# One opening load of an attention kernel issued from ScalarE's queue instead of SyncE's

## The chip, the cores and the metric

The kernel runs on one core of one Trainium2 chip. The metric is the device time of one execution in microseconds (us), given as the median of several executions. Times "at 2.73 us" are counted from the start of the profiled span. TensorE, which does the matrix multiplications, is called PE in the profile, VectorE DVE, ScalarE ACT, GpSimd POOL and SyncE SP. SPq and ACTq are the sequencers of SyncE and ScalarE, which issue loads; the 16 DMA engines then move a load's rows in packets, each engine a part of them. PSUM is the memory into which TensorE writes its results. PE begins at half its pace (two 256-column matmuls start 0.213 us apart, later 0.109), until the trace shows the full clock granted. ScalarE's "table load" brings in the tables for its functions. "Landing" is the time at which the last of a load's 16 semaphore events came in the trace, so that its reader may start.

## The reference, cut to what matters

Two independent problems, A and B, of the same shape (bf16 inputs; 32 query heads over 4 key/value heads):

```python
B, Sq, D = 16, 32, 1024            # 512 tokens of 1024 features
Hq, Hkv, Sk, Dh = 32, 4, 512, 128
q = (x @ wq)                       # 512 x 1024 times 1024 x 4096
scores = einsum("bhqd,bhkd->bhqk", q, k) * Dh ** -0.5
o = softmax(scores) @ v
out = o @ wo                       # A and B side by side
```

The case is about the first part of `x @ wq` of problem A alone. The contraction over 1024 features goes in eight chunks of 128; a chunk's weight rows are a 128 x 4096 matrix, of which one head takes 128 columns, or 256 bytes of each row.

## The kernel before: the opening

Six heads are begun first, chunk by chunk. x comes in as tokens by features and has to be transposed: chunks 0 to 3 by TensorE, the rest by transposing loads. All loads go through SyncE's queue.

```python
NF = REP - 2                       # 6 heads begun first; TT = 4 token tiles
nc.scalar.preload_act_table_set("natural_log_exp_and_others")
load_x(0, 0, TT // 2)              # x chunks 0-1, first half of the tokens, 128 KB
load_x(0, TT // 2, TT)             # ... second half, 128 KB
load_w0(0, 1, 0, NF // 2)          # chunk 0, heads 0-2, 96 KB   <- the load of the change
load_w0(0, 1, NF // 2, NF)         # chunk 0, heads 3-5, 96 KB
load_w0(1, 2, 0, NF)               # chunk 1, heads 0-5, 192 KB  ("chunk 1's rows")
load_x(2, 0, TT)                   # x chunks 2-3, 256 KB
load_w0(2, 3, 0, NF)               # chunk 2's rows
load_w0(3, 4, 0, NF)               # chunk 3's rows
...                                # more loads
warm_up(22)                        # 22 matmuls on constants, so that PE is not idle
for k, ts in enumerate(((0, TT // 2), (TT // 2, TT))):
    transpose_x(0, *ts, nc.vector.tensor_copy)
    transpose_x(1, *ts, nc.scalar.copy, spare[k])
for ts in ((0, TT // 2), (TT // 2, TT)):
    first_heads(range(0, NF // 2), (0,), *ts)      # six matmuls of 256 columns
first_heads(range(NF // 2, NF), (0,))              # three of 512 columns
first_heads(range(0, NF - 2), (1,))                # four of 512: wait for chunk 1's rows
transpose_x(2, 0, TT, nc.vector.tensor_copy)       # wait for x chunks 2-3
transpose_x(3, 0, TT, nc.scalar.copy)
...                                                # the rest of the kernel
```

## Time and profile before

| | before |
|---|---|
| time, median of 3 executions | 343.27 us (343.26 to 343.75) |
| span of the profiled execution | 341.4 us |
| PE busy | 335.0 us, 98% |
| only PE wait for a load in the opening that the page marks on a matmul | 0.4 us, for chunk 1's rows |

The page of the kernel before, its part 1 (busy time and share of the span) and the head of its part 4 (the chain of work that ended last, by engine):

```profile
PE 335.0 (98%) x2082; PEld 213.2 (62%) x2121; DVE 265.6 (78%) x336; ACT 185.8 (54%) x209; POOL 46.7 (14%) x206
...
PE 94%; DVE 1%; issue 1%; DMA 1%; SPq 1%; ACT 0%; POOL 0%; ACTq 0%
```

PE is busy almost throughout and makes up 94% of the chain, so only the few places where PE stands still can give time back. The next view is the chain of waits of the kernel before in its first 12 us, as start, length and what it was. L477 is the line that loads weight rows, L534 the first heads' matmuls, L524 the transposes of x.

```profile
1.75 0.46 SPq L477
...
2.25 0.43 SPq L477
...
2.73 3.29 DMA w_sb<-in_A_wq_dram
6.02 0.05 issue
6.07 1.04 PE q_ps L534 x4
7.11 0.45 PE xT_ps L524 x8
...
7.61 4.50 PE q_ps L534 x20
```

Read it backwards. The train of matmuls that starts at 7.61 hangs on the four matmuls at 6.07; these waited for a load issued at 2.73 (chunk 1's rows), which took 3.29 us to land, at 6.02. Ahead of it stand SyncE's issues, one after the other; the one at 1.75 is the load that the change moves. PE's own row of the timeline (start, length, what, count), merged over like instructions, for the kernel before:

```profile
3.24 1.06 PE L524 MATMUL xT_ps<-ident,x_sb 128*128 128x128 bf16 x8
4.10 1.60 PE L534 MATMUL q_ps<-xT,w_sb 128*128 128x256 bf16 x9
6.07 1.04 PE L534 MATMUL q_ps<-xT,w_sb 128*128 128x512 bf16 x4 [0.37 <-DMA w_sb<-in_A_wq_dram]
6.94 0.61 PE L524 MATMUL xT_ps<-ident,x_sb 128*128 128x128 bf16 x8
```

The merged row at 4.10 holds the nine matmuls of chunk 0. The ends of matmuls are modelled, so the row seems to end at 5.70; by the distance from start to start (0.216 us for 512 columns) the array is free at 5.54. Until 6.07 it waits 0.53 us. The row at 6.94, the transposes of x chunks 2-3: I call its start **M**.

What the 16 DMA engines did meanwhile, in stretches of half a microsecond (the last two figures of a row are the mean busy share of the DMA engines and the GB/s moved):

```profile
2.00:2.50 0.50, 0.50 (x8) 0.50 (x7) 0.00 (x0) 0.10 (x1) 0.00 (x0) 1.00 0.83 247
...
3.00:3.50 0.50, 0.50 (x8) 0.50 (x6) 0.00 (x0) 0.00 (x0) 0.00 (x0) 1.00 0.65 186
3.50:4.00 0.50, 0.50 (x8) 0.50 (x6) 0.29 (x1) 0.09 (x1) 0.00 (x0) 1.00 0.75 189
4.00:4.50 0.50, 0.50 (x6) 0.40 (x5) 0.29 (x1) 0.45 (x2) 0.00 (x0) 1.00 0.80 230
```

One load, chunk 1's rows, by its issue (engine, count, size, us from issue to landing):

```profile
w_sb<-in_A_wq_dram SPq DMA_DIRECT2D x1, 192.0 KB, 3.3
```

And the end of the kernel before: ScalarE's last copy of a result out of PSUM.

```profile
338.43 0.37 ACT L329 CAST o_sb<-f_ps 128x256 bf16<-128x256 f32 x1 [3.12 <-PE f_ps L320]
```

### The profile page before, as it was taken

Reading aid. Unit: us, or ns where it says so; the run is one execution under the profiler, and the core shown is the slowest. Engines: PE = TensorE matmul, PEld = TensorE weight load, DVE = VectorE, ACT = ScalarE, POOL = GpSimd, SP = SyncE. Lnnn points to the kernel's source line nnn. Section 1 sums busy time; section 2 is a strip of 40 time slices with the busy share of each in tenths; the row PEclk is TensorE's granted clock in tenths of the full one; section 3 lists DMA queues with packets and bytes.
Section 4 is the critical chain, followed back from the end, with each engine's and each line's share of the span. In section 5 each row is a group of like instructions: output and inputs, shape, how many; then the busy total and the mean of one; then the engine's idle time right before and its main releaser. Section 6 shows DMA issues by size and latency. Waiting matters only on the chain.

```text
span 341.4 us, 5454 instructions
## 1 busy us (share of the span) xinstructions
PE 335.0 (98%) x2082; PEld 213.2 (62%) x2121; DVE 265.6 (78%) x336; ACT 185.8 (54%) x209; POOL 46.7 (14%) x206
## 2 busy tenths in 40 slices
PE   8999999999999999999999999999999999999996
PEld 6455666666666666666666666666666666666555
DVE  1046988888988898888888988879888888889540
ACT  3058666666667667666645545555555555555110
POOL 0001110011111111110012221222122101111100
PEclk9999999999999999999999999999999999999999
DMA  6989999999999988999999956999449996340001
GB/s 192 289 166 286 287 219 241 192 198 276 302 282 203 232 231 221 212 302 288 325 274 266 276 135 142 335 256 250 117 109 292 355 206 160 95 113 10 18 18 33
DMA packets 128094, 71.70 MB, mean 210 GB/s; under 512 B 75840, under 2 KB 127296, under 8 KB 128064
## 3 DMA queue, kind: packets, MB, share of 16 engines
q1 hardware_dynamic: 127536, 70.21, 85.3%
q0 software_dynamic: 384, 1.05, 0.8%
q8 instruction: 17, 0.28, 0.3%
q14 instruction: 13, 0.11, 0.1%
q10 hardware_dynamic: 144, 0.07, 0.1%
HBM read 50.86 MB, written 2.10 MB: 155 GB/s over the span
## 4 chain that ended last, share of the span: by engine, by line
PE 94%; DVE 1%; issue 1%; DMA 1%; SPq 1%; ACT 0%; POOL 0%; ACTq 0%
PE f_ps L320 30%; PE q_ps L301 28%; PE ob L425 17%; PE s_ps L357 16%; PE q_ps L534 4%; DMA w_sb<-in_A_wq_dram 1%; DVE parts L376 1%; ACT p_sb L365 0%; SPq L465 0%; SPq L477 0%; DVE r L411 0%; DVE oT L447 0%; PE xT_ps L524 0%; DVE cs L384 0%; ACT o_sb L329 0%
## 5 line engine op out<-in xcount | busy, mean ns | idle before, releaser
L365 ACT ACTIVATE p_sb<-s_ps,shift 128x1024 bf16<-128x1024 f32 x128 | 142.6, 1114 | 97.7 <-PE s_ps L357 86.2
L376 DVE TRANSPOSE_TENSOR_REDUCE parts<-p_sb 128x32 f32<-128x1024 bf16 x128 | 158.7, 1240 | 21.0 <-ACT p_sb L365 19.3
L320 PE MATMUL f_ps<-wo_sb,oT 128*128 128x512 bf16 (+1 forms) x525 | 128.2, 366 | 0.6
L301 PE MATMUL q_ps<-xT,wq_sb 128*128 128x512 bf16 x430 | 113.3, 379 | 0.5
L425 PE MATMUL ob<-p_sb,v_sb 128*128 128x256 bf16 x512 | 76.8, 273 | 0.8
L357 PE MATMUL s_ps<-qT,kT 128*128 128x256 bf16 x512 | 76.8, 273 | 0.0
L320 PEld LDWEIGHTS <-oT 128*128 128x128 bf16 x544 | 53.2, 98 | 35.4
L357 PEld LDWEIGHTS <-kT 128*128 128x128 bf16 x512 | 56.9, 113 | 28.3
L301 PEld LDWEIGHTS <-wq_sb 128*128 128x128 bf16 x448 | 43.7, 98 | 32.4 <-DMA wq_sb<-in_A_wq_dram 0.4
L425 PEld LDWEIGHTS <-v_sb 128*128 128x128 bf16 x512 | 50.0, 98 | 20.1
L447 DVE TENSOR_TENSOR oT<-r,ob 128x512 bf16<-128x512 f32 x64 | 43.9, 686 | 19.9 <-PE ob L425 19.4
L411 DVE STREAM_TRANSPOSE r<-rall 128x512 f32<-128x512 f32 x64 | 44.2, 691 | 1.1
L309 ACT CAST qT<-q_ps 128x512 bf16<-128x512 f32 x56 | 32.6, 583 | 16.6 <-PE q_ps L301 16.6
L394 POOL COPY half<-cs 64x32 f32<-64x32 f32 x32 | 6.5, 204 | 232.0 <-DVE cs L384 232.0
L329 ACT CAST o_sb<-f_ps 128x512 bf16<-128x512 f32 (+1 forms) x17 | 9.5, 559 | 23.6 <-PE f_ps L320 23.6
L534 PE MATMUL q_ps<-xT,w_sb 128*128 128x512 bf16 (+1 forms) x65 | 14.2, 372 | 0.5 <-DMA w_sb<-in_A_wq_dram 0.4
L384 DVE TENSOR_REDUCE cs<-parts 128x32 f32<-128x128 f32 x32 | 12.1, 377 | 1.1
L406 DVE RECIPROCAL rall<-sums 128x32 f32<-128x32 f32 x32 | 10.2, 318 | 3.3 <-POOL sums L403 3.3
L534 PEld LDWEIGHTS <-w_sb 128*128 128x128 bf16 x67 | 6.4, 99 | 7.6 <-DMA w_sb<-in_A_wq_dram 0.9
L560 DVE CAST qT<-q_ps 128x512 bf16<-128x512 f32 x4 | 2.5, 684 | 10.2 <-PE q_ps L534 10.2
L331 POOL DMA_DIRECT2D out_dram<-o_sb x8 | 4.6, 574 | 29.3 <-ACT o_sb L329 29.3
L395 POOL TENSOR_TENSOR half<-half,cs 64x32 f32<-64x32 f32 x32 | 7.8, 242 | 2.6
(25 smaller groups left out, 44.8 us busy)
## 6 DMA issues: line engine op xcount, KB each, us to landing
v_sb<-in_A_v_cache_dram SPq DMA_DIRECT2D x16, 512.0 KB, 6.3
wq_sb<-in_B_wq_dram SPq DMA_DIRECT2D x8, 1024.0 KB, 5.9
wo_sb<-in_A_wo_dram SPq DMA_DIRECT2D x8, 1024.0 KB, 7.6
v_sb<-in_B_v_cache_dram SPq DMA_DIRECT2D x16, 512.0 KB, 4.6
wo_sb<-in_B_wo_dram SPq DMA_DIRECT2D x8, 1024.0 KB, 8.2
wq_sb<-in_A_wq_dram SPq DMA_DIRECT2D x5, 1024.0 KB, 6.6
wq_sb<-in_A_wq_dram SPq DMA_DIRECT2D x2, 512.0 KB, 7.4
kT<-in_A_k_cache_dram SPq DMA_TRANSPOSE x64, 4.4
```

Source lines behind the costliest of these rows:

```text
L301: nc.tensor.matmul(ps[:], lhsT=w[:, dc, (h % 4) * DH:(h % 4 + 1) * DH], rhs=xT[pr][:, dc, :], start=(dc == 0), stop=(dc == DC - 1),)
L309: nc.scalar.copy(out=qT[pr, g][:, :, hl, :], in_=ps[:].rearrange("p (b s) -> p b s", s=SQ),)
L320: nc.tensor.matmul(ps[:, 0:width], lhsT=oT[pr, tt][:, h, :], rhs=wo_tiles[pr, nh, h // REP][:, h % REP, off:off + width], start=(h == 0), ...
L357: nc.tensor.matmul(s_ps[:, c, :], lhsT=kT[:, i % GRP, c, :], rhs=qT[pr, g][:, b, :, :].rearrange("p h s -> p (h s)"), start=True, stop=True,)
L365: nc.scalar.activation(out=p_sb[:], in_=s_ps[:], func=ACTF.Exp, bias=shift[:], scale=SCALE)
L376: nc.vector.tensor_reduce(out=parts[k][:, q, :, :].rearrange("p c h -> p (c h)"), in_=st[i]["p"][:].rearrange("p c (h s) -> p (c h) s", s=SQ),
L384: nc.vector.tensor_reduce(out=cs[:], in_=parts.pop(k)[:].rearrange("p q c h -> p q h c"), axis=AX.X, op=ALU.add,)
L406: nc.vector.reciprocal(out=rall[:, k, :], in_=quad.pop(k)[:])
L411: nc.vector.transpose(out=r[:].rearrange("p n s -> p (n s)"), in_=rall[:, k, o * 2 * REP:(o + 1) * 2 * REP] .unsqueeze(2).to_broadcast([P, ...
L425: nc.tensor.matmul(ob[j][:, q, :], lhsT=v_sb[:, i % GRP, c, :], rhs=st[i]["p"][:, c, :], start=(c == 0), stop=(c == KC - 1),)
L447: nc.vector.tensor_tensor(out=out, in0=rcp.pop(j)[:].rearrange("p (q h) s -> p q h s", h=REP), in1=ob.pop(j)[:].rearrange("p q (h s) -> p ...
L534: nc.tensor.matmul(first_q[h][:, ts], lhsT=w0[dc // HC][:, dc % HC, h * DH:(h + 1) * DH], rhs=xT[0][:, dc, ts], start=(dc == 0 and t0 == 0 ...
```

## The change

SyncE issues its loads back to back, one each half microsecond. ScalarE issues nothing in the opening, and has only its table load to do before its first copy at 3.91 us. The change hands one load to ScalarE, so that all later ones leave SyncE one place earlier. ScalarE issues it ahead of its table load. It is the only load of the kernel outside SyncE's queue; SyncE, GpSimd and ScalarE also issue stores of results, at the end.

```diff
-            def load_w0(d0, d1, h0, h1):
-                nc.sync.dma_start(
+            def load_w0(d0, d1, h0, h1, eng=nc.sync):
+                eng.dma_start(
...
+            load_w0(0, 1, 0, NF // 2, nc.scalar)
             nc.scalar.preload_act_table_set("natural_log_exp_and_others")
             load_x(0, 0, TT // 2)
             load_x(0, TT // 2, TT)
-            load_w0(0, 1, 0, NF // 2)
             load_w0(0, 1, NF // 2, NF)
```

## The prediction

> **What bounds the kernel now.** TensorE: the page gives PE 335.0 us busy of a 341.4 us span (98%), and the chain of waits is 94% PE. The change touches only the first 8 us, so its worth is the PE idle time that loads cause there.
>
> **The opening, from the timeline, instruction by instruction.** SyncE issues loads back to back, one each 0.47 to 0.51 us: x chunks 0-1, first half at 0.74, second at 1.25, the three heads' rows at 1.75, the next three at 2.25, chunk 1's rows at 2.73, x chunks 2-3 at 3.20. They land at 3.09, 3.46, 4.02, 4.83, 6.02 and 6.84. PE warms up until 3.14, when x has just landed, transposes, and starts the first heads at 4.10. That start is set by the x copy out of PSUM (3.70 to 4.06) as much as by the moved load (4.02): making this load earlier alone gains nothing. The chain of waits runs through SyncE's five issues, then 3.29 us of DMA, chunk 1's rows: PE's last matmul before them is through at 5.54, the next starts at 6.07. That 0.53 us is the only PE idle time of note between 4.1 and 8 us; x chunks 2-3 arrive just in time.
>
> **What the change does.** By the instruction order, one 96 KB load leaves SyncE's queue for ScalarE's, ahead of the table load; nothing else changes.
> - Every later SyncE issue comes one pitch earlier, 0.47 to 0.50 us. Chunk 1's rows should land near 5.54, x chunks 2-3 near 6.37, and PE's train from 6.07 on should move by up to 0.48 us.
> - ScalarE: one issue of about 0.45 us before the table load (now ending at 2.10). Its first copy is at 3.91: slack remains.
> - Cost: the moved load's packets now travel together with x. The Trainium skill ("DMA: Bandwidth & Descriptors", Issuing engines are not separate DMA queues) says that loads from several engines share the same 16 DMA engines and only issue time is saved. The trace agrees that the engines are full from 2.2 to 2.8 us (about 300 GB/s). Estimate: x's first half lands 0.1 to 0.35 us later. PE idles a little after its warm-up; part is recovered, as PE runs at half pace until 4.2 anyway. Costs 0 to 0.15 of the 0.48 us.
>
> **Does it last?** From 9 to 18 us the DMA engines are full and SyncE's queue is blocked on them; that train starts earlier too, and PE from 7.6 us on hardly waits. I expect the gain to reach the end nearly whole.
>
> **Prediction.** About 0.4 us off, 342.9 us; range 342.4 to 343.5. Faster by over 2%: 0.005; within 2%: 0.99; slower by over 2%: 0.005.
>
> **What would show it.** Right: SyncE's issue of chunk 1's rows near 2.25 us; landing near 5.55; PE's 0.53 us wait near 0; the first q_ps to qT copy, now 17.75, near 17.3. Wrong: those rows landing still near 6.0 (bandwidth bound it); SyncE's issues after 1.25 us not earlier, or stretched.
>
> **What would make it wrong.** (a) "Perfetto Trace Analysis" (DMA Instruction — HWDGE) says that the descriptor generator is locked for exclusive use by one sequencer. If ScalarE's issue blocks SyncE's for its whole 0.45 us, the gain is zero and x's second half is late; no overlap of two issues stands in this trace. (b) x delayed enough to hold TensorE's clock-up back: up to 1 us slower. (c) A later load-bound point swallows the gain.

## The result, and the profile after

The changed kernel took 343.77 us (median of 6 executions, 343.37 to 344.32), the kernel before 343.37 us (6 executions, 343.26 to 343.82). The ratio is 1.001, 95% interval 0.9997 to 1.0023. A ratio is the mean time of one kernel's runs over that of the other's of the same rounds, so it is not quite the ratio of the medians. No gain shows, and the time lies above the range of the prediction.

The page of the changed kernel:

```profile
PE 335.3 (98%) x2082; PEld 213.7 (63%) x2121; DVE 265.6 (78%) x336; ACT 186.0 (54%) x209; POOL 46.7 (14%) x206
...
PE 97%; DMA 1%; issue 1%; ACT 0%; ACTq 0%
```

First what went as expected. The rows of SyncE's and ScalarE's sequencers in the timeline of the changed kernel:

```profile
0.74 0.96 SPq L465 DMA_DIRECT2D x_sb<-in_A_x_dram  x2
0.82 0.40 ACTq L477 DMA_DIRECT2D w_sb<-in_A_wq_dram  x1
...
1.75 0.93 SPq L477 DMA_DIRECT2D w_sb<-in_A_wq_dram  x2
2.73 0.43 SPq L465 DMA_DIRECT2D x_sb<-in_A_x_dram  x1
```

ScalarE issued its load from 0.82 to 1.22 us, while SyncE was issuing x from 0.74 on, and neither took longer for it. SyncE issued its next two loads from 1.75 on, chunk 1's rows at 2.25 (0.48 us earlier than before) and x chunks 2-3 at 2.73. Now the landing of chunk 1's rows:

```profile
w_sb<-in_A_wq_dram SPq DMA_DIRECT2D x1, 192.0 KB, 4.1
```

4.1 us instead of 3.3: issued at 2.25, they landed at 6.40, which is 0.38 us *later* than before. And PE no longer even waits for them. The chain of waits of the changed kernel in its first 12 us:

```profile
0.68 0.07 issue
0.74 3.10 DMA x_sb<-in_A_x_dram
3.84 0.05 issue
3.88 1.04 PE xT_ps L524 x8
4.92 2.64 PE q_ps L534 x13
7.56 0.45 PE xT_ps L524 x8
8.01 0.05 issue
8.06 4.07 PE q_ps L534 x18
```

The chain now starts with x's first half. It was issued at 0.74 as before, but took 3.10 us to land, at 3.84 instead of 3.09. From there PE itself is the chain: transposes, thirteen matmuls without a wait, transposes. PE's row of the timeline, to be held against the one of before:

```profile
3.88 1.04 PE L524 MATMUL xT_ps<-ident,x_sb 128*128 128x128 bf16 x8 [0.44 <-DMA x_sb<-in_A_x_dram]
4.71 2.85 PE L534 MATMUL q_ps<-xT,w_sb 128*128 128x256 bf16 x13
7.40 0.61 PE L524 MATMUL xT_ps<-ident,x_sb 128*128 128x128 bf16 x8
```

The warm-up is through at 3.24 and x is there at 3.84, so PE stands still for 0.64 us that it did not lose before (the profile counts 0.44, as the last warm-up matmul's modelled end is later). The nine matmuls of chunk 0 and the four of chunk 1 follow without a gap, and M is 7.40 instead of 6.94. The windows of the changed kernel tell where x was:

```profile
2.00:2.50 0.50, 0.50 (x8) 0.50 (x7) 0.00 (x0) 0.50 (x1) 0.00 (x0) 1.00 0.40 119
...
3.00:3.50 0.50, 0.45 (x5) 0.18 (x2) 0.00 (x0) 0.00 (x0) 0.00 (x0) 1.00 1.15 349
3.50:4.00 0.50, 0.12 (x2) 0.12 (x3) 0.00 (x0) 0.00 (x0) 0.00 (x0) 1.00 0.71 165
4.00:4.50 0.50, 0.50 (x7) 0.50 (x6) 0.18 (x1) 0.00 (x0) 0.00 (x0) 1.00 0.42 91
```

In the half microsecond after 2.00, when x alone had got 247 GB/s, x and the moved load together got 119. By 3.50 this was made up (349 instead of 186 in the row at 3.00). Then less was moved again: 165 instead of 189 in the row at 3.50, and 91 instead of 230 in the one at 4.00. The last copy of the changed kernel:

```profile
338.83 0.37 ACT L329 CAST o_sb<-f_ps 128x256 bf16<-128x256 f32 x1 [3.12 <-PE f_ps L320]
```

From M to this copy it takes 331.49 us in the kernel before (338.43 less 6.94) and 331.43 in the changed one. So after M nothing changed: the 0.4 us come from the opening alone. (The prediction's own mark, the first q_ps to qT copy, came at 18.21 us instead of 17.75; the prediction had 17.3.)

### The profile page after: what moved, and what is told of

Same layout as the page of the kernel before. It is cut to its first block, busy times and chain, and to the rows that moved or that the text cites. A ratio compares the mean times of both kernels' runs of the same rounds, so it can differ in the third digit from the quotient of the medians.

```text
span 341.8 us, 5454 instructions
## 1 busy us (share of the span) xinstructions
PE 335.3 (98%) x2082; PEld 213.7 (63%) x2121; DVE 265.6 (78%) x336; ACT 186.0 (54%) x209; POOL 46.7 (14%) x206
## 4 chain that ended last, share of the span: by engine, by line
PE 97%; DMA 1%; issue 1%; ACT 0%; ACTq 0%
PE f_ps L320 32%; PE q_ps L301 28%; PE ob L425 17%; PE s_ps L357 16%; PE q_ps L534 4%; DMA x_sb<-in_A_x_dram 1%; PE xT_ps L524 0%; ACT o_sb L329 0%; ACTq L329 0%
```

## The experiments

Four batches of four kernels, each batch on one chip beside the kernel before. The names of the theories in the expectations:

- **I**, of the prediction: when chunk 1's rows are *issued* decides when they land.
- **A**: the moved load, travelling together with x, delays x.
- **D**: what the DMA engines can *deliver* decides when chunk 1's rows land, whenever they are issued.
- **H** (formed later): it is rows of 1,536 bytes that land late.
- **Gap theory**: PE's idle gap keeps its clock down for another period.

The landing and clock times of the profiled execution of each kernel. "Clock full" is the time from which the trace's record of granted clock has the full value; the distance from start to start of the first heads' 256-column matmuls is 0.213 us ahead of it and 0.109 after it.

| kernel | x first half lands | chunk 1's rows: issued, land | clock full | M | ratio to before (95%) |
|---|---|---|---|---|---|
| before | 3.09 | 2.73, 6.02 | 4.36 | 6.94 | |
| before_again | 2.98 | 2.73, 6.35 | 5.93 | 7.27 | 0.9999 (0.9986 to 1.0012) |
| after | 3.84 | 2.25, 6.40 | 5.77 | 7.40 | 1.001 (0.9997 to 1.0023) |
| after_again | 3.82 | 2.25, 6.18 | 6.79 | 7.89 | 1.0034 (1.0018 to 1.0049) |
| extra_768 | 3.82 | 2.73, 6.63 | 4.25 | 7.66 | 1.0035 (1.0022 to 1.0048) |
| extra_64 | 3.39 | 2.73, 6.01 | 5.28 | 6.93 | 1.0015 (1.0003 to 1.0028) |
| merged | 3.20 | 2.25, 5.90 | 4.92 | 7.54 | 1.0012 (0.9999 to 1.0024) |
| late_first | 3.77 | 2.25, 6.13 | 7.17 | 8.06 | 0.9997 (0.9984 to 1.001) |
| late_second | 3.85 | 2.26, 6.29 | 5.36 | 7.27 | 1.0031 (1.0013 to 1.005) |
| held_first | 2.94 | 2.25, 5.42 | 4.82 | 6.88 | 1.0023 (0.9999 to 1.0046) |
| held_first_again | 3.15 | 2.25, 5.56 | 4.30 | 7.24 | 1.0006 (0.9992 to 1.0019) |
| held_second | 3.25 | 2.25, 5.92 | 4.82 | 7.34 | 1.0013 (0.9999 to 1.0027) |
| before_warm15 | 3.13 | 2.73, 6.16 | 5.61 | 7.08 | 1.001 (0.9996 to 1.0023) |
| after_warm29 | 3.88 | 2.25, 6.59 | 5.78 | 7.51 | 1.0011 (0.9997 to 1.0024) |

(split_chunk1, chunk1_two, cut_1024 and rows_2048 cut the load of chunk 1's rows or size it otherwise; they are told below.) All kernels gave correct results.

The landings of chunk 1's rows, sorted by their issue and by whether a 768-byte-row load travelled beside x, separate the two effects. Issued at 2.73 with x alone, as in before, before_again and before_warm15, they landed at 6.02 to 6.35; at 2.25 with x alone (merged, both held_first, held_second) at 5.42 to 5.92; at 2.25 beside the collision (after, after_again, after_warm29, late_first, late_second) at 6.13 to 6.59; at 2.73 beside the collision (extra_768) at 6.63. (The 64-byte rows of extra_64 left them at 6.01.) The groups are small and their kernels differ in other ways too, but they don't overlap where it matters: the earlier issue is worth some 0.5 us on average, and the collision costs some 0.6, which takes it back.

The times of five kernels (extra_768, extra_64, split_chunk1, chunk1_two, cut_1024) hold a cost that has nothing to do with the opening. Each has one DMA issue more than the 176 of the kernel before, and its span ends 3.42 to 3.49 us after the start of the last copy; with 176 issues it is 2.99 to 3.01, with the 175 of merged 3.07. The last store lands alike in all, 2.01 to 2.09 us after that start. But of the waits with which SyncE closes the program, one is still to be gone through then in the kernels with 176 issues, two in merged and eight in these five. Take some 0.4 us off the times of the five to compare openings, or compare M.

### Both kernels once more: before_again, after_again

No edit.

> The kernel before once more, unchanged, to see which marks of the opening repeat. If the opening is deterministic: x's first half lands at 3.1 us, chunk 1's rows at 6.0, TensorE's granted clock goes to full at 4.4 us, and the last head-0 matmul train starts at 7.6 us, each within 0.1. If the two differ between executions of one kernel, the difference of 0.4 us between the two kernels may be chance; then landing or clock-up times here move by 0.3 us or more.

> The changed kernel once more, unchanged. Theory A (the moved load delays x's first half): x's first half lands at 3.8 us again, chunk 1's rows at 6.4, the clock goes to full late, near 5.8, and the time is 0.2 to 0.7 us over that of before. Rival (chance in one execution): x lands near 3.1 to 3.4 or the clock goes up near 4.4, and the time is under that of before.

Measured: before_again 343.36 us, after_again 344.22 us, before beside them 343.33. x's landing repeats to a tenth in both kernels, 3.1 and 2.98 against 3.84 and 3.82: chance does not explain x, as theory A had it. The rest of the opening is not deterministic: in one and the same kernel the clock became full at 4.36 or at 5.93, and chunk 1's rows landed at 6.02 or at 6.35. The expectation that all of before's marks would repeat within 0.1 us was wrong.

The late clock costs time where PE is what the chain runs through. The first heads' matmuls with 256 columns (group by form in the stretch from 3.8 to 7.5 us; count, busy us and mean ns) of the kernel before and, below, of after_again:

```profile
L534 PE MATMUL q_ps<-xT,w_sb 128*128 128x256 bf16 x6 | 1.0, 300 | 0.0
```

```profile
L534 PE MATMUL q_ps<-xT,w_sb 128*128 128x256 bf16 x6 | 1.5, 421 | 0.0
```

In before the clock came at 4.36, and most of the six ran at the short duration; in after_again it came at 6.79, and all six took 421 ns. M there was 7.89.

### A useless load beside x: extra_768 and extra_64

```diff
+            nc.scalar.dma_start(
+                out=rall[:].rearrange("p j n -> p (j n)").bitcast(BF16)[:, 0:384],  # 0:32 in extra_64
+                in_=wq_v[:, 0, 0:384],
+            )
             nc.scalar.preload_act_table_set("natural_log_exp_and_others")
```

The target is a tile that is first needed some 30 us later. SyncE's queue is left as it was.

> The kernel before, with a useless load of the same source rows and the same shape (128 rows of 768 B) issued by ScalarE where the change puts its load; SyncE's queue stays whole. Theory A (travelling together with x is what delays x): x's first half lands near 3.8 us, TensorE's clock goes to full near 5.8, and as all later loads are issued at their old times and 96 KB more have to move, the time is 0.5 to 1.2 us over before. Rival (the delay comes of taking the load out of SyncE's queue, by other semaphores or another order): x lands at 3.1 us and the time is within 0.2 us of before.

> As the run with the useless 768 B rows, but of 64 B rows: as many descriptors (128), a twelfth of the bytes (8 KB). If it is bytes that x loses to, x's first half lands within 0.1 us of 3.1 and the time within 0.2 us of before. If it is the making of descriptors for two queues at a time, or the second queue itself, x lands at 3.4 us or later, near the 768 B case.

Measured: extra_768 344.54 us, extra_64 343.70, before 343.33; some 0.4 us of each excess stand at the end of the program (see above). The landing of x's first half, by its issue, in extra_768 and, below, in extra_64:

```profile
x_sb<-in_A_x_dram SPq DMA_DIRECT2D x1, 128.0 KB, 3.1
```

```profile
x_sb<-in_A_x_dram SPq DMA_DIRECT2D x1, 128.0 KB, 2.6
```

With the 768-byte rows x lands at 3.82, just as in the changed kernel, though no load left SyncE's queue. That is theory A: x's delay needs the load beside it and nothing else of the change. With 64-byte rows it lands at 3.39; in the eleven profiles in which nothing was issued beside x, it landed between 2.92 and 3.25. So both causes seem to have a share: 8 KB on a second queue cost x 0.14 us against the latest of the eleven and some 0.3 us against their mean, and the other 88 KB 0.43 us more. This speaks against "bytes alone" and against "the second queue alone", but extra_64 was profiled once. Its time, 0.37 us over before, is no evidence for either: M was 6.93, as in the kernel before, and the excess lies at the program's end. The gap that x's delay leaves need not make the clock late: in extra_768 PE was idle from 3.24 to 3.87, and the clock was full at 4.25.

### The earlier issue without a second queue: merged

```diff
-            load_w0(0, 1, 0, NF // 2)
-            load_w0(0, 1, NF // 2, NF)
+            load_w0(0, 1, 0, NF)
```

> The kernel before with the two loads of chunk 0's weight rows made one (six heads, 192 KB), all on SyncE: chunk 1's rows are issued one pitch earlier (2.25 instead of 2.73 us) with no second queue. Theory I, of the prediction (the time of issue decides when chunk 1's rows land): they land near 5.55 us. Theory D (what has to be delivered ahead of them decides): they land between 5.9 and 6.4 as in both runs of before, and the earlier issue gains nothing. The first heads now wait for 192 KB (landing 4.5 to 4.9), so under D the time is 0 to 0.5 us over before; under I up to 0.3 us under it.

Measured: 343.98 us, before 343.44. Chunk 1's rows landed at 5.90: on the edge of theory D's range, well after the 5.55 of theory I. The first heads had to wait until 5.32 for the larger load (expected 4.5 to 4.9), so this kernel could not gain.

### Behind the table load: late_first and late_second

```diff
-            load_w0(0, 1, 0, NF // 2, nc.scalar)
             nc.scalar.preload_act_table_set("natural_log_exp_and_others")
+            load_w0(0, 1, 0, NF // 2, nc.scalar)     # late_first, against the changed kernel
```

In late_second ScalarE issues heads 3 to 5 in the same place, and SyncE keeps heads 0 to 2.

> The changed kernel with ScalarE's load behind the table load, so issued near 2.1 us instead of 0.82 and out of x's way. Theory A (the loss is x's delay): x's first half is back at 3.0 to 3.1 us and its second at 3.5 to 3.7, and the loss is gone. Under theory D chunk 1's rows still land at 5.9 to 6.4 and the time is within 0.3 us of before; under theory I they land near 5.55 and the time is 0.3 to 0.4 us under before. Rival to A (a load on ScalarE costs whenever it is issued): still 0.4 us or more over before.

> As the run before it, but ScalarE issues the second three heads' rows (needed near 4.9 us) and SyncE keeps the first three. x and the first three heads land as in before (3.1, 3.5 to 3.7, 4.0). D: chunk 1's rows land at 5.9 to 6.4, time within 0.2 us of before. I: near 5.55, and the time 0.3 to 0.5 us under before.

Measured: late_first 343.49 us, late_second 344.15, before 343.44. Neither is the experiment that it was meant to be. ScalarE's rows of the timeline in late_first:

```profile
0.82 1.28 ACT L482 ACT_TABLE_LOAD   x1 [0.82 <-PEq L694]
0.85 0.38 ACTq L477 DMA_DIRECT2D w_sb<-in_A_wq_dram  x1
```

The load stands behind the table load in the program and was issued at 0.85 us all the same, while the table load was running. So late_first has the changed kernel's schedule to 0.03 us, and x landed at 3.77 (3.85 in late_second). Both are repeats of the collision. late_first was as fast as before in four of five executions (343.31 to 343.49) and took 344.38 in the fifth, the profiled one, whose clock was full only at 7.17.

### Out of x's way: held_first, twice

```diff
+            nc.gpsimd.memset(w0[0][:, 0, 0:NF // 2 * DH], 0.0)
             load_w0(0, 1, 0, NF // 2, nc.scalar)
```

The load must wait for the fill of its target by GpSimd, and so was issued at 1.78 us. SyncE's issues stay at the changed kernel's times.

> The repair of the run whose load did not wait behind the table load: the changed kernel, with GpSimd first filling the target of ScalarE's load with zeros, so that the load has to wait and is issued near 1.6 to 2.0 us, when x's packets are nearly through. Theory A: x's first half is back at 3.0 to 3.2 us. Theory D: chunk 1's rows land at 5.9 to 6.4 although issued at 2.25, and the time is within 0.3 us of before. Theory I: they land near 5.55, time 0.3 to 0.5 us under before. If x is still at 3.8, theory A is wrong.

> The held load once more, unchanged. If the 5.42 us landing of chunk 1's rows was typical, they land below 5.7 again and the first transposes of x chunks 2-3 start below 7.0; if it was chance, they land at 5.9 to 6.4. x's first half lands at 2.9 to 3.2 in either case. Executions of 345 us or more may turn up again, as TensorE is idle from 4.0 to 4.6.

Measured: 343.45 us both times, before 343.35 and 343.43; two of the six executions of held_first took 345.29 and 345.68, of which more below. x is back at 2.94 and 3.15: theory A once more. And chunk 1's rows, issued at 2.25 as in the changed kernel, now landed at 5.42 and 5.56. In held_first:

```profile
w_sb<-in_A_wq_dram SPq DMA_DIRECT2D x1, 192.0 KB, 3.2
```

3.2 us against the 4.1 of the changed kernel. This is what theory I had forecast (5.55), and theory D in its plain form, "whenever they are issued", is refuted. It is the collision with x that kept them back in the changed kernel (merged, with no collision and 5.90, lies between). The windows of held_first:

```profile
2.00:2.50 0.50, 0.50 (x8) 0.50 (x7) 0.00 (x0) 0.31 (x1) 0.00 (x0) 1.00 0.73 217
...
4.00:4.50 0.50, 0.31 (x3) 0.04 (x1) 0.29 (x1) 0.43 (x2) 0.00 (x0) 1.00 0.96 267
```

The trace's packets tell when the bytes were lost: not at the start. By 3.5 us the changed kernel's four with the collision had moved 364 to 380 KB, more than the 332 to 339 of the three with the loads of before. They fell behind from 3.5 to 4.5 us, with 81 to 152 KB against 152 to 191, and 240 and 248 in held_first and its repeat. Why the DMA engines moved so little just then, the trace does not tell. By 5.5 us the three profiles with the loads of before (before, before_again, before_warm15) had moved 753, 703 and 742 KB; the changed kernel's four with the collision (after, after_again, late_first, after_warm29) 734, 762, 748 and 736; held_first and its repeat 863 and 851. So the earlier issue is worth about 124 KB by then (857 less 733, the means), half a microsecond of delivery at the 240 GB/s of that stretch, and in these four the collision takes all of it. But the bytes are not the whole account: late_second, a collision too, had moved 802 KB by 5.5 us (and 206 GB/s from 2.0 to 2.5), and yet its x landed at 3.85 and its chunk 1's rows at 6.29.

Why then is held_first no faster? The chain of waits of held_first:

```profile
1.78 2.74 DMA w_sb<-in_A_wq_dram
4.52 0.14 issue
4.66 2.39 PE q_ps L535 x13
7.05 0.45 PE xT_ps L525 x8
```

Now the load that was moved is itself late: issued at 1.78, it shares the way with SyncE's load of heads 3 to 5 and lands at 4.52 (4.94 in the repeat) instead of 4.02, and PE waits for it. The gain at one load is paid at another. M was 6.88 and 7.24.

### The load that has most time, held: held_second

```diff
+            for _ in range(2):
+                nc.gpsimd.memset(w0[0][:, 0, NF // 2 * DH:NF * DH], 0.0)
+            load_w0(0, 1, NF // 2, NF, nc.scalar)
             nc.scalar.preload_act_table_set("natural_log_exp_and_others")
...
-            load_w0(0, 1, NF // 2, NF)
```

> The second three heads' rows (needed at 4.87 us) on ScalarE, held by two fills of its target to an issue near 2.2 us; SyncE keeps x and the first three heads and issues chunk 1's rows at 2.25. x lands at 2.9 to 3.2, the first three heads at 4.0 to 4.2, so that TensorE has no gap. If early landings as in held_first are typical, chunk 1's rows land at 5.4 to 5.7 and the time is 0.2 to 0.5 us under before, with no slow executions; by theory D they land at 5.9 to 6.4 and the time is within 0.2 us of before.

Measured: 343.92 us, before 343.43. x landed at 3.25 and the first three heads at 4.11, undisturbed. But ScalarE's load, issued at 2.26, landed at 5.70 instead of 4.83, and PE waited for it (idle from 5.13 to 5.83); chunk 1's rows landed at 5.92, on the edge of theory D's range. The forecast gain did not come. No use of ScalarE's queue that I tried beats the kernel before.

### Cutting chunk 1's rows: split_chunk1, chunk1_two, cut_1024, rows_2048

All issue from SyncE alone. The loads from chunk 1's rows on:

```diff
 split_chunk1:
-            load_w0(1, 2, 0, NF)
+            load_w0(1, 2, 0, NF - 2)
             load_x(2, 0, TT)
+            load_w0(1, 2, NF - 2, NF)
 chunk1_two:
-            load_w0(1, 2, 0, NF)
+            load_w0(1, 2, 0, NF - 2)
+            load_w0(1, 2, NF - 2, NF)
 cut_1024:
-            load_w0(1, 2, 0, NF)
+            load_w0(1, 2, 0, NF - 2)
             load_x(2, 0, TT)
-            load_w0(2, 3, 0, NF)
-            load_w0(3, 4, 0, NF)
+            load_w0(1, HC, NF - 2, NF)
+            load_w0(2, 3, 0, NF - 2)
+            load_w0(3, 4, 0, NF - 2)
 rows_2048:
-            load_w0(1, 2, 0, NF)
+            load_w0(1, 2, 0, REP)
             load_x(2, 0, TT)
-            load_w0(2, 3, 0, NF)
-            load_w0(3, 4, 0, NF)
-            load_w0(0, HC, NF, REP)
+            load_w0(2, 3, 0, REP)
+            load_w0(3, 4, 0, REP)
+            load_w0(0, 1, NF, REP)
```

> The kernel before with chunk 1's rows cut at the point where TensorE leaves them: heads 0 to 3 (128 KB), then x chunks 2-3, then heads 4 and 5. No issue is earlier, one is added. D in terms of bytes: the first part has 64 KB less to deliver, at the 160 GB/s that the opening delivers some 0.4 us, so it lands near 5.6 and the time is 0.2 to 0.5 us under before. Rival (the slowest of the 16 engines takes its time whatever the size): it lands at 6.0 or later, and the time is that of before or over it.

> The kernel before with chunk 1's rows as two loads, heads 0 to 3 (1,024 B rows) and then 4 and 5 (512 B rows), both ahead of x chunks 2-3: the same bytes in the same order, one more issue. Theory D (bytes ahead decide): the second part lands at 6.0 to 6.4 as the whole did. Theory H (rows of 1,536 B are slow to deliver, with one late engine): the first part lands near 5.25 and the second near 5.5 to 5.7, although its issue is one pitch later.

> A version meant to win: chunks 1 to 3 in rows of 1,024 B for heads 0 to 3 (one load each), heads 4 and 5 of all three chunks in one load of 512 B rows, put behind x chunks 2-3; one issue more than before. H: chunk 1's first part at 5.25, x chunks 2-3 at 6.2, the 192 KB of heads 4 and 5 by 7.0, chunk 2's rows by 7.5: the second transposes start at 6.45 and the train behind them is held up by less than 0.3 us, so the time is 0.2 to 0.5 us under before. Rival D: chunk 2's rows land after 8.0, and the time is over before.

> The kernel before with chunks 1 to 3 loaded as whole 2,048 B rows (eight heads, 256 KB each), and only chunk 0's heads 6 and 7 apart: as many issues as before, but 64 KB more ahead of x chunks 2-3. H (it is the 1,536 B rows that are slow): chunk 1's rows land by 5.9 with a spread under 0.6 us over the engines, and the time is within 0.2 us of before or under it. D: they land at 6.4 to 6.8, and the time is 0.3 to 0.8 us over before.

Measured: split_chunk1 344.12 us (ratio 1.0018, 1.0005 to 1.0031), chunk1_two 344.13 (1.0021, 1.0008 to 1.0034), cut_1024 343.80 (1.001, 0.9997 to 1.0023), rows_2048 343.70 (1.0008, 0.9995 to 1.0021). The cuts did bring chunk 1's first part in at 5.24 to 5.43 us, as H had it, and in chunk1_two its second part at 5.42. But the lateness moved on. In split_chunk1 M was 6.45, the best of all, and then PE stood until 8.35 for chunk 2's rows (landed 8.30 instead of 7.34). In cut_1024 M was 6.50, and PE stood until 7.97 for the same. In chunk1_two x chunks 2-3 landed at 7.85 instead of 6.84, and M was 7.90. In rows_2048 chunk 1's rows of 2,048 bytes landed at 6.37, spread over 1.1 us among the 16 engines' events, which H had excluded. So H as stated is refuted. Without the 0.4 us at the program's end, cut_1024 would be about even with before (343.35) and split_chunk1 and chunk1_two some 0.3 us over it. In each kernel the opening's loads arrive with little to spare, and what one gets earlier another pays for. Which DMA engine is the late one, and why, the trace does not tell; that stays open.

### The gap in PE's work: before_warm15, after_warm29

```diff
-            warm_up(22)
+            warm_up(15)      # against the kernel before; warm_up(29) against the changed one
```

> The kernel before with 15 warm-up matmuls in place of 22: TensorE is idle from 2.4 to 3.1 us, a gap as long as the one of the changed kernel, and no load changes. Gap theory: some executions show the late clock, 345 us or more (about one in six, so 0 to 3 of 6). Rival (the slow executions come of the loads on two queues): all lie between 343.1 and 343.9, as before's do. x lands at 3.0 to 3.1 and chunk 1's rows at 6.0 to 6.4 in either case.

> The changed kernel with 29 warm-up matmuls in place of 22, which fill TensorE's wait for x up to 3.88 us; no load changes. Gap theory: no execution over 345 us. Rival: such executions still turn up. x lands at 3.8 and chunk 1's rows at 6.0 to 6.4; the time is 0 to 0.9 us over before, as TensorE gains nothing that the load of chunk 1's rows does not take back.

Measured: 343.53 us (343.31 to 344.32) and 343.70 us (343.66 to 344.14), before 343.43. With the gap of before_warm15 no execution went to 345 us, and with the filled gap of after_warm29 none did either, five executions each (one of before_warm15, at 344.32, went over the 343.9 that the rival allowed). That settles nothing about the executions of 345.3 to 345.9 us. Over the study, 5 of 54 executions of kernels whose ScalarE issues a load in the opening were such, and none of 83 of kernels that load from SyncE alone, whose longest was 344.67. So they came only with the second queue, but none of them was profiled, and their cause stays open. Filling the gap did not help the changed kernel: x chunks 2-3 then landed at 7.42, and M was 7.51.

## Why the prediction was wrong

Point by point, in the words of the prediction:

1. *"Every later SyncE issue comes one pitch earlier"*: right. Chunk 1's rows were issued at 2.25 us.
2. *"(a) ... If ScalarE's issue blocks SyncE's for its whole 0.45 us"*: did not happen. The issues overlapped (0.82 to 1.22 on ScalarE, 0.74 to 1.19 on SyncE).
3. *"Estimate: x's first half lands 0.1 to 0.35 us later"*: this is the term that was mis-sized. It landed 0.75 us later in the pair of profiles (3.84 less 3.09), and in all six profiles with 768-byte rows beside it at 3.77 to 3.88. The estimate shared out a full rate of about 300 GB/s between two loads. But the pair did not get that rate: 119 GB/s from 2.0 to 2.5 us, where x alone had 247. (In late_second the pair got 206 and x was as late, so the low rate is not the whole cause; that part stays open.)
4. *"Chunk 1's rows should land near 5.54"*: the failed step. They landed at 6.40, 6.18, 6.13 and 6.59 in four profiles of that schedule. That an earlier issue brings an earlier landing was not wrong: with the same issue and no collision they landed at 5.42, 5.56, 5.90 and 5.92. What failed is the overlap: the prediction booked the collision's cost to x alone, and chunk 1's rows, behind x, pay it as well. I had costed it at 0 to 0.15 us; it took the whole 0.48.
5. *"part is recovered, as PE runs at half pace until 4.2 anyway"*: wrong in assuming that the clock comes at 4.2. The Trainium skill ("TensorE: Matmul & The Clock Gate", Part 1) says that the window of the clock's monitor is 3,413 ns and runs freely, so that the point of change is not fixed to the kernel's start; the runs agree: the kernel before alone had 4.36 and 5.93 us, all profiles 4.25 to 7.17, and their stretches at full clock lasted 337.92 or 334.51 us, which lie 3.41 apart. A late clock cost nothing where a load came late anyway (before_again: clock full at 5.93, chunk 0 through at 6.35, just as chunk 1's rows landed), and its full price where PE was the chain (after_again against after: clock 1.02 us later, M 0.49 us later, at half the pace). In the first profile of the kernel before PE waited 0.53 us for chunk 1's rows, which hid a good deal. With x 0.64 to 0.90 us late nothing is left to hide behind.
6. *"(b) x delayed enough to hold TensorE's clock-up back"*: not shown, and not excluded. The clock was full at 4.25 with x late (extra_768) and at 5.93 with x in time (before_again). But the four profiles of the changed kernel's loads have 5.77, 5.78, 6.79 and 7.17, and of the other fourteen only before_again comes later than 5.61. Among the four is after_warm29, whose gap was filled (5.78).
7. *"I expect the gain to reach the end nearly whole"*: there was no gain, but that what happens in the opening reaches the end is right. From M to the last copy it takes 331.43 to 331.49 us in sixteen of the eighteen profiles (split_chunk1 and cut_1024 wait for chunk 2's rows after M). Rival (c) falls.

All executions taken together fit point 5, but do not prove it. Some executions have a mean granted clock of 0.998 or 0.999 instead of 1.000; the two of the changed schedule that bear the mark and were profiled had their clock full at 6.79 and 7.17, the latest of all. I take the mark as a sign of a late clock. That is an inference, and not a safe one: in all four marked profiles it comes of the clock's fall just before the end of the span (at 341.29 and 341.68 in these two), as the record does not count the slow start. In extra_768 and chunk1_two, whose spans are longer, an early clock (4.25 and 4.27) bears the mark too, and before_again (5.93) does not. So the mark may also follow from a longer time instead of causing it. The medians (before: its executions in the four batches and before_again, as no clock is on record for its first six; changed: after, after_again and late_first, whose schedule is the same to 0.03 us):

| | mean granted clock 1.000 | below 1.000 |
|---|---|---|
| before | 343.35 us (40 executions) | 343.79 us (7) |
| changed | 343.49 us (10) | 344.32 us (7) |

By these the change costs some 0.1 us in executions without the mark and 0.5 us in those with it; all together the medians are 343.36 and 343.99 us. Read as clock, it would also explain why this schedule differed between the batches (1.001, 1.0034, 0.9997): 2 of 6, 4 of 6 and 1 of 5 of its executions bear the mark.

## What to carry to other kernels

Here a second issuing queue saved 0.48 us of issue time, and the collision of its load took it back. If its load starts together with the one load that the first computation waits for, the two get in each other's way, so look at what starts beside it, and count what its own load then loses. Holding the load back, and moving one that is needed later, were both tried here, and neither beat the kernel before. When landing times grow down the queue (2.35 us for the first load here, 3.29 for the fifth, 3.64 for the sixth, which are also larger), the loads seem to stand behind one another, and one that comes earlier is paid for by another. A gain of 0.1% in an opening has to be looked for in the landing times of several profiles: the clock's start alone seems to move the time by about as much. And a test kernel with one load more can pay for it where nobody looks, here 0.4 us at the program's end: compare marks inside the trace, not times alone.

## What the Trainium skill lacked or had wrong

- "DMA: Bandwidth & Descriptors" (Issuing engines are not separate DMA queues) says that loads from several engines interleave and that only issue time is saved. The runs agree, but the page has no cost of the collision: two queues started 0.08 us apart moved 119 GB/s in the stretch from 2.0 to 2.5 us in which one had moved 247, and the first load landed 0.75 us later; 8 KB in 64-byte rows on the second queue were enough, in one profile, for a landing at 3.39 us, against 2.92 to 3.25 without.
- "Perfetto Trace Analysis" (DMA Instruction — HWDGE) says that the descriptor generator is locked for exclusive use. In the trace two issues on SyncE and ScalarE overlapped for 0.37 us (0.82 to 1.19) and took 0.45 and 0.40 us, while SyncE's took 0.45 alone in the kernel before (no load of ScalarE was issued alone; its last store's issue took 0.38); a wait for a lock does not show in the issue times. Whether it is part of the slow start of the two loads is open.
- "TensorE: Matmul & The Clock Gate" (Part 1) gives the point of change a variation of 500 ns either way, with a free-running window of 3,413 ns. Here two profiles of the kernel before had 4.36 and 5.93 us, 1.57 apart, and all profiles range over 2.9 us, which is still less than one free-running window.
